# A fused attention and two-layer feed-forward kernel: GpSimd's subtractions and normalisations moved to VectorE in halves, another spacing of the y forms, and another order of the tail's joins

## The chip, the cores and the metric

The kernel runs on one core of a Trainium2 chip. A core has TensorE (PE in the profile: matmul; PEld: its weight load), VectorE (DVE), ScalarE (ACT), GpSimd (POOL) and SyncE (SP), which here issues the DMA transfers. Each engine works through its own queue in program order and waits on semaphores for the others. The metric is the device time of one execution in microseconds (us), as the median of several runs.

## What is computed

```python
# attention: q, k, v of shape (8 batches, 8 heads, 576 rows, 64)
q_s = softmax of q over the 64 columns of a row
k_s = exp(k - max over the 576 rows), divided by its sum over the rows
kv  = einsum('bhsd,bhse->bhde', k_s, v)
x   = einsum('bhsd,bhde->bhse', q_s, kv)      # -> 4608 tokens x 512
# first layer
g, val = x @ w_gate, x @ w_val                # 512 -> 1536
y = (g * sigmoid(g) * val) @ w_out            # 1536 -> 512
# second layer
h = y @ w_in                                  # 512 -> 1024
solu = h * softmax(h)
out = (layernorm(solu) * g_ln) @ w_out2       # 1024 -> 512
```

Each float32 product is made of three matmuls of a high and a low part (lines 938 to 940 of the kernel before).

## The kernel before

The work has three parts. A **prologue** does the attention of the first batch. Then nine **blocks** of 512 tokens run the first layer. Block 0 also converts the weights as they arrive. In blocks 1 to 7 the order of the work is written by hand: TensorE's products of a block are numbered in gaps, three for each n (12 matmuls each): gap 3n is the gate product of feature tile n (`wg`), gap 3n+1 the output product of tile n-2 (`y<-a,wo`), gap 3n+2 the value product of tile n (`wv`). `tasks_of(j)` says ahead of which gap every other task of the block is issued. Last come 18 **pairs** of the second layer, each with seven products of block matrices in the order 1, 6, 5, 2, 7, 3, 4 (`emit_pair`), whose sums are put together on VectorE.

Beside the products of tile n there are three steps: ScalarE's sigmoid form `st` from `wg` (L971), VectorE's product `st` with `wv` (L976), and the split into a high part on ScalarE (`a`, L980) and a low part on VectorE (`a`, L982). The text calls them st(n) and a(n). The product `y<-a,wo` of tile n needs a(n).

Beside them a block prepares the next batch and stores y:

- k, in two groups of four heads (`kv_max_rows` L511, `kv_max_all` L523 to L545, `kv_exp` L606, `kv_mm` L615). VectorE finds the column maxima and spreads them (`mt`, L539); the subtraction `kt - mt` (L545) is done by GpSimd in four pieces of 96x384; ScalarE's exp needs another function table than its sigmoid, so a table load stands ahead of it. The subtraction stands at gaps 5 and 20, the exp at 9 and 24, the matmuls `pk` at 11 and 26.
- q (`q_max` L685 and L688 at gap 8, `q_exp` L696 at 12, `q_norm` L702 to L708 at 14, `q_turn` at 18). Reductions are VectorE's, the subtraction (L688) and the normalisation (L708) GpSimd's, four pieces of 128x512 each. Later `q_split` (L761, L766) makes `qhl`, and `x_mm` (`px`, L786 to L788) the x of the next block.
- y in seven forms (`y_form`): some are sums of quarters of y (`yz`, L902, VectorE), each is split into a high part (ScalarE, L920) and a low part (VectorE, L922) in a tile `yf` with two buffers, and stored (L924). They start at gaps 5, 6, 12, 13, 14, 15, 16.
- one of the second layer's weights: `join_w2` (L320, L324) at gap 23.

In the tail, `h_first` copies product 1 from PSUM (`c`, L1343, ScalarE), `h_u` and `h_w` add products 6 and 5 to it (`uw`, L1347 and L1351), `h_other` makes `hh` (L1358). `emit_join_low` and `emit_join_high` put a transposed tile together again after its DMA (`zt<-wT`, L1430 on VectorE, L1433 on ScalarE), `emit_parts` splits it (L1441 ScalarE, L1444 VectorE), `emit_store` scales the output (L1481).

Of the kernel before, what the change touches and what calls it, by code (L numbers as in the profile page):

```python
# [19 lines left out]
P = 128  # L20
# [28 lines left out]
class Task:  # L49
# [7 lines left out]
    def step(self):  # L57
        before, Task.current = Task.current, self
        try:
            if self.g is None:  # L60
                self.g = self.f(*self.a)
                if self.g is None:
                    self.done = True
                    return None
            return next(self.g)
        except StopIteration:
            self.done = True
            return None
        finally:
            Task.current = before  # L70

    def finish(self):
        while not self.done:
# [132 lines left out]
def attention_glu_solu_kernel(  # L206
# [46 lines left out]
    def f32(ap):  # L253
        return ap.bitcast(F32)
# [18 lines left out]
            for t in kv_parts[b, p]:  # L273
                nc.gpsimd.memset(f32(t), 0.0)

    yf_dram = dram.tile([NT2 // 2, P, 2, 7, 2 * P], F32, name="yf_dram")
    NS = 8
    w1_dram = dram.tile([NS, P, 2, 2, DM], F32, name="w1_dram")
    x2_dram = dram.tile([KD, P, DF2], F32, name="x2_dram")
# [213 lines left out]
            )  # L493
        vt_t[b, h0] = vt

    def pieces(eng, start, stop):

        n = 1 if eng is nc.gpsimd else stop - start
        return [slice(x, x + n) for x in range(start, stop, n)] if n else []

    km_t, kt_exp, kt_sub = {}, set(), set()

    def kv_max(pool, b, h0, split=0):
        kv_max_rows(pool, b, h0)
        kv_max_all(pool, b, h0, split)

    def kv_max_rows(pool, b, h0):
        raw = kt_t[b, h0][0]
# [3 lines left out]
                out=m, in0=m if c > 1 else raw[:, 0], in1=raw[:, c], op=ALU.max  # L512
            )

    def kv_max_all(pool, b, h0, split=0):

        raw, kt = kt_t[b, h0]
        m = km_t.pop((b, h0))
        kt_sub.add((b, h0))
        N = HG * D  # L520
        NQ = SP // 32
        r = stat.tile([SP, N // 32], F32, tag="r", bufs=1, name="r")
        nc.vector.tensor_reduce(  # L523
            out=r, in_=m.rearrange("p h (e j) -> p (h e) j", j=32), axis=AX.X, op=ALU.max,
            apply_transpose=True,
        )
        r2 = stat.tile([32, N // 32, NQ], F32, tag="r2", bufs=1, name="r2")
        for a in range(NQ):
            nc.vector.tensor_copy(out=r2[:, :, a], in_=r[32 * a:32 * (a + 1), :])
        r3 = stat.tile([32, N // 32], F32, tag="r3", bufs=1, name="r3")  # L530
        nc.vector.tensor_reduce(out=r3, in_=r2, axis=AX.X, op=ALU.max)
        mb = tmp.tile([SP, N // 32, 32], F32, tag="st", bufs=3, name="mb")
        for a in range(NQ):
            nc.vector.tensor_copy(
                out=mb[32 * a:32 * (a + 1)],
                in_=r3.rearrange("p (n o) -> p n o", o=1).to_broadcast([32, N // 32, 32]),
            )
        mt = stat.tile([SP, 1, HG, D], F32, tag="m", bufs=1, name="mt")
        nc.vector.transpose(  # L539
            out=mt.rearrange("p o h d -> p (o h d)"), in_=mb.rearrange("p n j -> p (n j)")  # L540
        )
        yield
        for eng, s in ((nc.vector, slice(0, split)), (nc.gpsimd, slice(split, HG))):
            for s in pieces(eng, s.start, s.stop):
                eng.tensor_tensor(  # L545
                    out=kt[:, :, s, :], in0=raw[:, :, s, :],
                    in1=mt[:, :, s, :].to_broadcast([SP, KC, s.stop - s.start, D]),
                    op=ALU.subtract,
                )

    kT_t, kx_t = {}, {}

# [123 lines left out]
            need(q_at.get((j, h), 0) == n - 1)  # L676
            q_at[j, h] = n

    def q_max(pool, j, hs, eng=nc.gpsimd):
        q_step(j, hs, 1)  # L680
        placed(qt_t, j)
        raw, qt = (t[:, :, hs, :] for t in qt_t[j])
        n, nc_, nh = qt.shape[:3]
        qm = stat.tile([n, nc_, nh, 1], F32, tag="qm", bufs=2, name="qm")
        nc.vector.tensor_reduce(out=qm[:, :, :, 0], in_=raw, axis=AX.X, op=ALU.max)  # L685
        yield d["km"]
        for s in pieces(eng, 0, nc_):
            eng.tensor_tensor(  # L688
                out=qt[:, s], in0=raw[:, s],
                in1=qm[:, s].to_broadcast([n, s.stop - s.start, nh, D]), op=ALU.subtract,  # L690
            )

    def q_exp(j, hs):
# [1 line left out]
        qt = qt_t[j][1][:, :, hs, :]  # L695
        nc.scalar.activation(out=qt, in_=qt, func=AF.Exp)  # L696

    def q_norm(pool, j, hs, eng=nc.gpsimd):
        qt = qt_t[j][1][:, :, hs, :]
        n, nc_, nh = qt.shape[:3]  # L700
        qs = stat.tile([n, nc_, nh, 1], F32, tag="qs", bufs=2, name="qs")
        nc.vector.tensor_reduce(out=qs[:, :, :, 0], in_=qt, axis=AX.X, op=ALU.add)  # L702
        nc.vector.tensor_scalar_add(out=qs, in0=qs, scalar1=1e-9)
        nc.vector.reciprocal(out=qs, in_=qs)
        q_step(j, hs, 3)
        yield d["km"]
        for s in pieces(eng, 0, nc_):
            eng.tensor_tensor(  # L708
                out=qt[:, s], in0=qt[:, s],
                in1=qs[:, s].to_broadcast([n, s.stop - s.start, nh, D]), op=ALU.mult,  # L710
            )

    qT_t = {}
# [102 lines left out]
    def tasks_of(j):  # L816

        t = {}
        b = j + 1
        if b < B:
            for n, (load, rows, sub, exp, mm) in enumerate(((0, 2, 5, 9, 11), (12, 17, 20, 24, 26))):
                h0 = n * HG
                if n:
                    at(t, load, kv_load, att, b, h0)
                    at(t, load, v_load, att, b, h0)  # L830
                at(t, rows, kv_max_rows, att, b, h0)
                at(t, sub, kv_max_all, att, b, h0)
                at(t, exp, kv_exp, b, h0)
                for u in range(2):
                    at(t, mm, kv_mm, ps_at, att, b, h0, u)
        at(t, 15, lambda: w2_raw[j - 1].start())
        at(t, 23, join_w2, j - 1)
        at(t, 24, parts_of_w2, j - 1)
        if j + 1 < NB:
            at(t, 8, q_max, att, j + 1, ALLH)  # L840
            at(t, 12, q_exp, j + 1, ALLH)
            at(t, 14, q_norm, att, j + 1, ALLH)
            at(t, 18, q_turn, att, j + 1)
            at(t, 24, x_tiles, ph1x, j + 1)
            for p in range(NPAIR):
                at(t, 27 + p, q_split, att, j + 1, p)
                at(t, 29 + p, x_mm, ps_at, j + 1, p)
            at(t, 27, kv_next, j + 1)
            at(t, 33, q_next, j + 1)
        y_forms_at(t, j - 1)  # L850
        for e, f in enumerate(STREAM):
            if f is not None:
                at(t, 3 * f + 2, stream_next, j, e)
        at(t, 24, store_w2, j - 1)
        at(t, 25, stream_next, j, STREAM.index(None))
        return t
# [49 lines left out]
    def y_form(j, n):  # L906


        i, x, with_ = Y_FORMS[n]
        of = lambda n, r: y_quarter(j, n, r)  # L910
        if with_:
            if x and with_[0]:
                yz[j] = att.tile([P, 2, KH, P], F32, tag="z", bufs=1, name="yz")
            y_sum(yz[j], of, x, with_)
            s = yz[j]
        else:
            s = of(*x)
        f = att.tile([P, 2, 2, KH * P], F32R, tag="qhl", bufs=2, name="yf")
        h, l = (f[:, n].rearrange("p q (k t) -> p q k t", k=KH) for n in range(2))
        nc.scalar.copy(out=h, in_=s)  # L920
        yield
        nc.vector.tensor_tensor(out=l, in0=s, in1=f32(h), op=SUB)  # L922
        for q in range(2):
            nc.sync.dma_start(out=yf_dram[2 * j + q, :, :, i], in_=f32(f[:, :, q]))  # L924

    def y_forms_at(t, j):


        tasks = [Task(y_form, (j, n)) for n in range(7)]
        for n, g in enumerate((5, 6, 12, 13, 14, 15, 16)):  # L930
            at(t, g, tasks[n].step)
            at(t, g + 1, tasks[n].finish)

# [345 lines left out]
    def y_load(p):  # L1279
# [2 lines left out]

        for n in range(2):
            nc.sync.dma_start(
                out=f32(yq[p][n]).rearrange("p i k t -> p (i k t)"),
                in_=yf_dram[p, :, n].rearrange("p i w -> p (i w)"),
            )

    def y_make(p, n):
# [11 lines left out]
        f = tmp.tile([P, 2, KH, P], F32R, tag="st", bufs=3, name="yf")  # L1301
        nc.scalar.copy(out=f[:, 0], in_=s)
        nc.vector.tensor_tensor(out=f[:, 1], in0=s, in1=f32(f[:, 0]), op=SUB)
        nc.sync.dma_start(out=yf_dram[p, :, :, i], in_=f32(f).rearrange("p n k t -> p n (k t)"))

    t = tasks_of(NB - 1)
    at(t, 0, x_load)
# [190 lines left out]
    def emit_pair(p):  # L1498
# [6 lines left out]
        if p == 2:  # L1505
            h_first(p)
            emit_join_low(a)
            emit_join_high(a)
        if p > 1:
            emit_store(a - 1)  # L1510
            emit_parts(a, 0)
        if p == 0 or p > 2:
            h_first(p)
        product(p, 6)
        if p > 1:
            emit_join_low(b)
            emit_join_high(b)
        h_u(p)
        if p == 1:
            emit_join_low(a)  # L1520
            emit_join_high(a)
        product(p, 5)
        if p > 1:
            emit_parts(a, 1)
            emit_parts(b, 0)
        h_w(p)
        product(p, 2)
        h_11(p)
        product(p, 7)
# [109 lines left out]
```

## Time and profile before

| | |
|---|---|
| median of 3 runs | 1392.57 us (1392.31 to 1393.76) |
| the profiled execution | 1392.51 us, of which 1390.6 us from the first to the last instruction |
| TensorE busy | 1348.8 us (97%), weight loads 1110.7 us (80%) |
| VectorE busy | 835.2 us (60%) |
| ScalarE busy | 691.2 us (50%) |
| GpSimd busy | 164.6 us (12%) |
| mean granted TensorE clock | 0.988 of full speed |

A share is an average over the whole span. An engine with a small share can still be the one that another waits for at some place. TensorE's 97% leaves some 42 us in which it is idle, and the larger part of them lies in the prologue and in block 0: it is busy for 71.73 of the first 100 us.

### The profile page before, as it was taken

What the parts mean: (1) busy time and instruction counts of PE and PEld (TensorE: products, weight loads), DVE (VectorE), ACT (ScalarE), POOL (GpSimd) and SP (SyncE); (2) the same over time, 40 slices, a digit from 0 to 9 for tenths busy, and PEclk for the clock granted to TensorE, in tenths of its full rate; (3) what the DMA queues carried; (4) which work ended last, traced back from release to release, by engine and by line L of the source; (5) the groups of instructions that cost most, each with busy time, mean ns of one, the idle gap of its engine ahead of it and who ended that gap; (6) DMA issues with size and microseconds to landing.
All of it is one profiled execution on the core that took longest, in us unless ns stands there. A gap on an engine that the chain in (4) does not pass through costs nothing. (4 is left out here: it accounts for less than half of the span.)

```text
span 1390.6 us, 17771 instructions
## 1 busy us (share of the span) xinstructions
PE 1348.8 (97%) x6705; PEld 1110.7 (80%) x6705; DVE 835.2 (60%) x1407; ACT 691.2 (50%) x963; POOL 164.6 (12%) x196
## 2 busy tenths in 40 slices
PE   7769999999999999999999999999999999999998
PEld 6558888888888788888888788888887888888887
DVE  5868746446446545545645625445287787787774
ACT  5766434435434425425525524433157666667764
POOL 4000023022021121122112102000000000000000
PEclk8979999999999999999999999999999999999999
DMA  9983676756856656665666664656546766766651
GB/s 272 279 283 90 173 212 153 186 174 163 173 174 165 164 169 174 174 175 167 172 192 162 197 182 153 181 170 209 181 138 165 204 176 170 184 182 180 167 128 47
DMA packets 280741, 245.49 MB, mean 177 GB/s; under 512 B 210640, under 2 KB 257232, under 8 KB 269904
## 3 DMA queue, kind: packets, MB, share of 16 engines
q1 hardware_dynamic: 280656, 244.36, 62.6%
q8 instruction: 53, 0.87, 0.3%
q14 instruction: 32, 0.26, 0.1%
HBM read 162.01 MB, written 57.15 MB: 158 GB/s over the span
## 5 line engine op out<-in xcount | busy, mean ns | idle before, releaser
L980 ACT CAST a<-st 128x512 fp32r<-128x512 f32 x108 | 66.9, 620 | 274.6 <-DVE st L976 273.8
L976 DVE TENSOR_TENSOR st<-st,wv 128x512 f32<-128x512 f32 x108 | 73.8, 683 | 211.7 <-PE wv L940 208.5
L938 PE MATMUL wg<-xh,wgv 128*128 128x512 f32 x432 | 172.4, 399 | 12.1 <-ACT wgv L335 11.5
L939 PE MATMUL wg<-xl,wgv 128*128 128x512 f32 x432 | 170.3, 394 | 0.9 <-DVE xl L793 0.9
L939 PE MATMUL y<-a,wo 128*128 128x512 f32 x432 | 169.1, 391 | 2.1 <-DVE a L982 2.1
L938 PE MATMUL y<-a,wo 128*128 128x512 f32 x432 | 169.0, 391 | 1.9 <-ACT a L980 1.9
L940 PE MATMUL wg<-xh,wgv 128*128 128x512 f32 x432 | 170.0, 394 | 0.8 <-DVE wgv L345 0.7
L940 PE MATMUL y<-a,wo 128*128 128x512 f32 x432 | 168.7, 391 | 0.0
L938 PE MATMUL wv<-xh,wgv 128*128 128x512 f32 x432 | 168.5, 390 | 0.0
L940 PE MATMUL wv<-xh,wgv 128*128 128x512 f32 x432 | 168.1, 389 | 0.0
L939 PE MATMUL wv<-xl,wgv 128*128 128x512 f32 x432 | 168.1, 389 | 0.0
L982 DVE TENSOR_TENSOR a<-st,a 128x512 fp32r<-128x512 f32 x108 | 78.7, 728 | 71.9 <-ACT a L980 71.8
L1473 PE MATMUL y<-w,zhl 128*128 128x512 f32 (+1 forms) x296 | 113.6, 384 | 0.0
L1475 PE MATMUL y<-w,zhl 128*128 128x512 f32 (+1 forms) x296 | 113.5, 383 | 0.0
L1474 PE MATMUL y<-w,zhl 128*128 128x512 f32 (+1 forms) x296 | 113.5, 383 | 0.0
L938 PEld LDWEIGHTS wg<-xh,wgv 128*128 128x128 f32 x432 | 82.2, 190 | 30.2 <-ACT wgv L335 11.9
L545 POOL TENSOR_TENSOR kt<-kt,mt 96x384 f32<-96x384 f32 x48 | 61.2, 1302 | 358.8 <-DVE mt L539 358.8
L971 ACT ACTIVATE st<-wg 128x512 f32<-128x512 f32 x108 | 64.5, 597 | 72.8 <-PE wg L940 72.5
L940 PEld LDWEIGHTS wg<-xh,wgv 128*128 128x128 f32 x432 | 82.1, 190 | 19.2 <-DVE wgv L345 1.9
L938 PEld LDWEIGHTS y<-a,wo 128*128 128x128 f32 x432 | 81.5, 189 | 19.4 <-ACT a L980 2.7
L939 PEld LDWEIGHTS y<-a,wo 128*128 128x128 f32 x432 | 81.5, 189 | 19.3 <-DVE a L982 2.7
L939 PEld LDWEIGHTS wg<-xl,wgv 128*128 128x128 f32 x432 | 82.4, 191 | 17.9 <-DVE xl L793 1.7
(264 smaller groups left out, 2557.7 us busy)
## 6 DMA issues: line engine op xcount, KB each, us to landing
wgv<-w_dram SPq DMA_DIRECT2D x64, 1024.0 KB, 5.3
yf_dram<-yf SPq DMA_DIRECT2D x126, 256.0 KB, 2.8
yh<-yf_dram SPq DMA_DIRECT2D x18, 896.0 KB, 4.8
yl<-yf_dram SPq DMA_DIRECT2D x18, 896.0 KB, 6.8
vt<-in_v_dram SPq DMA_DIRECT2D x64, 144.0 KB, 4.5
out_dram<-ot SPq DMA_DIRECT2D x35, 256.0 KB, 2.9
w_dram<-wgv SPq DMA_DIRECT2D x8, 1024.0 KB, 8.3
kt<-in_k_dram SPq DMA_DIRECT2D x56, 144.0 KB, 5.6
```

Of the source, the lines that this page charges most:

```text
L545: eng.tensor_tensor(out=kt[:, :, s, :], in0=raw[:, :, s, :], in1=mt[:, :, s, :].to_broadcast([SP, KC, s.stop - s.start, D]), op=ALU.subtract,)
L938: nc.tensor.matmul(out=po, lhsT=wh, rhs=rh, start=start, stop=False, **k)
L939: nc.tensor.matmul(out=po, lhsT=wh, rhs=rl, start=False, stop=False, **k)
L940: nc.tensor.matmul(out=po, lhsT=wl, rhs=rh, start=False, stop=stop, **k)
L971: nc.scalar.activation(out=st, in_=pg, func=AF.Silu)
L976: nc.vector.tensor_tensor(out=st, in0=st, in1=pv, op=ALU.mult)
L980: nc.scalar.copy(out=ah, in_=st)
L982: nc.vector.tensor_tensor(out=al, in0=st, in1=f32(ah), op=ALU.subtract)
L1473: nc.tensor.matmul(out=po[:, s], lhsT=zh[:, c, :], rhs=wh[:, s], start=first, stop=False)
L1474: nc.tensor.matmul(out=po[:, s], lhsT=zh[:, c, :], rhs=wl[:, s], start=False, stop=False)
L1475: nc.tensor.matmul(out=po[:, s], lhsT=zl[:, c, :], rhs=wh[:, s], start=False, stop=last)
```

## The change

Five parts:

- **k.** The subtraction of a group is done by VectorE in two halves (96 partitions x 768 elements each), both one gap after the maxima, gaps 6 and 21.
- **q.** In blocks the subtraction and the normalisation are VectorE's too, each in two halves of 128x1024: the subtraction at gaps 9 and 10, the sums at 13, the normalisation at 14 and 15.
- **The prologue's q** stays on GpSimd, with one instruction of 128x4x256 where there were four of 128x256.
- **y forms** start at gaps 4, 6, 8, 11, 12, 14, 16. A form is stored by one transfer of 512 KB where there were two of 256 KB; `yf_dram` is laid out anew, and `y_load` of the tail reads seven runs of 1 KB for each partition where it read one of 7 KB.
- **Tail.** `h_first` stands ahead of `emit_parts` and `emit_store`, `emit_store` behind `emit_parts`; the join of b stands behind `h_u` and product 5 (for pair 2 behind `h_w` too).

```diff
-    yf_dram = dram.tile([NT2 // 2, P, 2, 7, 2 * P], F32, name="yf_dram")
+    yf_dram = dram.tile([NB, 7, P, 2, 2, 2 * P], F32, name="yf_dram")
...
-        for eng, s in ((nc.vector, slice(0, split)), (nc.gpsimd, slice(split, HG))):
-            for s in pieces(eng, s.start, s.stop):
-                eng.tensor_tensor(
-                    out=kt[:, :, s, :], in0=raw[:, :, s, :],
-                    in1=mt[:, :, s, :].to_broadcast([SP, KC, s.stop - s.start, D]),
-                    op=ALU.subtract,
-                )
+        for s in range(0, HG, step):
+            s = slice(s, s + step)
+            nc.vector.tensor_tensor(
+                out=kt[:, :, s, :], in0=raw[:, :, s, :],
+                in1=mt[:, :, s, :].to_broadcast([SP, KC, step, D]), op=ALU.subtract,
+            )
...
-                at(t, sub, kv_max_all, att, b, h0)
+                a = Task(kv_max_all, (att, b, h0))
+                at(t, sub, a.next)
+                at(t, sub + 1, a.finish)
...
-            at(t, 8, q_max, att, j + 1, ALLH)
+            m = Task(q_max, (att, j + 1, ALLH, nc.vector, 2))
+            n = Task(q_norm, (att, j + 1, ALLH, nc.vector, 2))
+            at(t, 8, m.next)
+            at(t, 9, m.next)
+            at(t, 10, m.finish)
             at(t, 12, q_exp, j + 1, ALLH)
-            at(t, 14, q_norm, att, j + 1, ALLH)
+            at(t, 13, n.next)
+            at(t, 14, n.next)
+            at(t, 15, n.finish)
...
-        for q in range(2):
-            nc.sync.dma_start(out=yf_dram[2 * j + q, :, :, i], in_=f32(f[:, :, q]))
+        nc.sync.dma_start(out=yf_dram[j, i], in_=f32(f))
...
-        for n, g in enumerate((5, 6, 12, 13, 14, 15, 16)):
+        for n, g in enumerate((4, 6, 8, 11, 12, 14, 16)):
...
-                out=f32(yq[p][n]).rearrange("p i k t -> p (i k t)"),
-                in_=yf_dram[p, :, n].rearrange("p i w -> p (i w)"),
+                out=f32(yq[p][n]).rearrange("p i k t -> p i (k t)"),
+                in_=yf_dram[p // 2, :, :, n, p % 2].rearrange("i p w -> p i w"),
...
             emit_join_high(a)
+            emit_parts(a, 0)
+        elif p > 2:
+            h_first(p)
+            emit_parts(a, 0)
+        elif p == 0:
+            h_first(p)
         if p > 1:
             emit_store(a - 1)
-            emit_parts(a, 0)
-        if p == 0 or p > 2:
-            h_first(p)
         product(p, 6)
-        if p > 1:
-            emit_join_low(b)
-            emit_join_high(b)
         h_u(p)
...
         product(p, 5)
+        if p == 2:
+            h_w(p)
         if p > 1:
+            emit_join_low(b)
+            emit_join_high(b)
             emit_parts(a, 1)
             emit_parts(b, 0)
-        h_w(p)
+        if p != 2:
+            h_w(p)
```

TensorE's order is the same in both kernels. What moves stands in the queues of VectorE, ScalarE, GpSimd and SyncE. Three places follow; a line number is that of the kernel the row is from.

VectorE in block 3, from the low part of the third y form to the second normalisation half, before (L976 and L982 are st(4) and a(4), then L702 to L704 the sums of q):

```order
L922 TENSOR_TENSOR yf<-yt,yf 128x512
L902 TENSOR_TENSOR yz<-yt 128x512
L976 TENSOR_TENSOR st<-st,wv 128x512
L982 TENSOR_TENSOR a<-st,a 128x512
L702 TENSOR_REDUCE qs<-qt 128x32
L703 TENSOR_SCALAR qs<-qs 128x32
L704 RECIPROCAL qs<-qs 128x32
L922 TENSOR_TENSOR yf<-yz,yf 128x512
L902 TENSOR_TENSOR yz<-yz,yt 128x512
```

The same place in the change (L980 and L986 are st(4) and a(4), L699 to L701 the sums of q, L706 the normalisation halves, L907 `yz`, L927 `yf`):

```order
L907 TENSOR_TENSOR yz<-yt 128x512
L927 TENSOR_TENSOR yf<-yz,yf 128x512
L907 TENSOR_TENSOR yz<-yz,yt 128x512
L699 TENSOR_REDUCE qs<-qt 128x32
L700 TENSOR_SCALAR qs<-qs 128x32
L701 RECIPROCAL qs<-qs 128x32
L927 TENSOR_TENSOR yf<-yz,yf 128x512
L980 TENSOR_TENSOR st<-st,wv 128x512
L986 TENSOR_TENSOR a<-st,a 128x512
L706 TENSOR_TENSOR qt<-qt,qs 128x1024
L907 TENSOR_TENSOR yz<-yt,yz 128x512
L706 TENSOR_TENSOR qt<-qt,qs 128x1024
```

The sums of q and one form now stand ahead of st(4) and a(4), and the normalisation halves stand behind a(4), between forms. Between these and a(5) there follow one `yf`, one `yz` and st(5).

VectorE in block 3 at the second k group, before (L539 makes `mt`; L976 and L982 are st(7) and a(7)):

```order
L534 COPY mb<-r_3626 32x256 x3
L539 STREAM_TRANSPOSE mt<-mb 96x256
L976 TENSOR_TENSOR st<-st,wv 128x512
L982 TENSOR_TENSOR a<-st,a 128x512
L320 SCALAR_TENSOR_TENSOR w2r2r<-w2r2r 128x1024
```

and in the change (L543 is the subtraction):

```order
L532 COPY mb<-r_3571 32x256 x3
L537 STREAM_TRANSPOSE mt<-mb 96x256
L543 TENSOR_TENSOR kt<-kt,mt 96x6x128 x2
L980 TENSOR_TENSOR st<-st,wv 128x512
L986 TENSOR_TENSOR a<-st,a 128x512
L323 SCALAR_TENSOR_TENSOR w2r2r<-w2r2r 128x1024
```

The two halves stand between `mt` and st(7). Ahead of this place, from a(5) to `mt`, VectorE's rows are the same in both: the row maxima of k, a `yf`, a copy `qw`, st(6), a(6), and the steps from the maxima to `mt`.

VectorE in pair 2 of the tail, before (L1430 are the joins of a and b, L1347 is `h_u`, L1351 `h_w`, L1358 `hh`):

```order
L1430 COPY zt<-wT 128x1024 x2
L1347 TENSOR_TENSOR uw<-c_8164,h 128x512
L1444 TENSOR_TENSOR zhl<-zt,zhl 128x1024
L1351 TENSOR_TENSOR uw<-uw,h 128x512
L1358 TENSOR_TENSOR hh<-uw,h 128x512
```

and in the change (L1434 joins, L1351 `h_u`, L1355 `h_w`, L1362 `hh`):

```order
L1434 COPY zt<-wT 128x1024
L1351 TENSOR_TENSOR uw<-c_8044,h 128x512
L1355 TENSOR_TENSOR uw<-uw,h 128x512
L1434 COPY zt<-wT 128x1024
L1448 TENSOR_TENSOR zhl<-zt,zhl 128x1024
L1362 TENSOR_TENSOR hh<-uw,h 128x512
```

Both sums stand ahead of the second join now, which waits for a DMA; the first `hh` still stands behind a split of the joined tile.

## Rows read from the trace of the kernel before

**Rows 1.** Busy time of each engine in a stretch, granted clock, DMA share, GB/s.
```profile
100.00:1034.00 934.00, 927.07 (x4705) 767.80 (x4704) 496.86 (x835) 396.39 (x565) 130.94 (x117) 1.00 0.61 171
```

**Rows 2.** TensorE's waits: engine line <- releaser, us in total, times, longest.
```profile
PE wg L938 <- ACT wgv L335: 11.5, 1, 11.5
PE pk L615 <- ACT kt L606: 6.1, 6, 1.6
...
PE y L724 <- POOL qt L708: 2.5, 1, 2.5
...
PE h L938 <- DVE hh L1358: 1.3, 3, 0.9
...
PE h L938 <- DVE uw L1347: 0.9, 1, 0.9
...
PE h L938 <- ACT c L1343: 0.7, 2, 0.5
...
PE px L787 <- DVE qhl L766: 0.5, 2, 0.3
```

**Rows 3.** Timeline around block 3's second k group: start, duration, [idle before <- releaser].
```profile
450.84 0.44 DVE L539 STREAM_TRANSPOSE mt<-mb 96x256 f32<-96x256 f32 x1
451.21 0.65 DVE L976 TENSOR_TENSOR st<-st,wv 128x512 f32<-128x512 f32 x1
...
451.36 5.37 POOL L545 TENSOR_TENSOR kt<-kt,mt 96x384 f32<-96x384 f32 x4 [15.41 <-DVE mt L539]
...
452.42 0.59 ACT L971 ACTIVATE st<-wg 128x512 f32<-128x512 f32 x1
453.03 1.28 ACT L606 ACT_TABLE_LOAD   x1
456.76 1.48 ACT L606 ACTIVATE kt<-kt 96x1536 f32<-96x1536 f32 x1 [2.45 <-POOL kt L545]
...
456.28 0.39 PE L940 MATMUL wv<-xh,wgv 128*128 128x512 f32 x1
458.30 1.74 PE L615 MATMUL pk<-vt,kt 96*64 96x65 f32 x48 [1.63 <-ACT kt L606]
```

**Rows 4.** TensorE's timeline behind that wait.
```profile
459.97 0.80 PE L938 MATMUL wg<-xh,wgv 128*128 128x512 f32 x1
...
463.40 0.39 PE L940 MATMUL wg<-xh,wgv 128*128 128x512 f32 x1
```

**Rows 5.** Timeline of block 3 between the y forms and a(5).
```profile
424.53 0.68 DVE L902 TENSOR_TENSOR yz<-yt 128x512 f32<-128x512 f32 x1
...
426.67 0.69 DVE L982 TENSOR_TENSOR a<-st,a 128x512 fp32r<-128x512 f32 x1 [0.74 <-ACT a L980]
427.28 2.28 DVE L702 TENSOR_REDUCE qs<-qt 128x32 f32<-128x2048 f32 x1
...
430.74 1.41 DVE L902 TENSOR_TENSOR yz<-yz,yt 128x512 f32<-128x512 f32 x1
...
441.07 0.62 ACT L920 CAST yf<-yz 128x512 fp32r<-128x512 f32 x1 [3.68 <-DMA yf_dram<-yf]
...
442.24 0.69 DVE L982 TENSOR_TENSOR a<-st,a 128x512 fp32r<-128x512 f32 x1 [2.80 <-ACT a L980]
...
442.99 0.51 PE L939 MATMUL y<-a,wo 128*128 128x512 f32 x1 [0.22 <-DVE a L982]
```

**Rows 6.** VectorE's subtraction of a whole k group in the first blocks, grouped by shape.
```profile
L545 DVE TENSOR_TENSOR kt<-kt,mt 96x1536 f32<-96x1536 f32 x2 | 3.5, 1754 | 0.1
```

**Rows 7.** TensorE around the first `px` of block 5.
```profile
680.29 0.39 PE L940 MATMUL wv<-xh,wgv 128*128 128x512 f32 x1
...
682.18 0.45 PE L938 MATMUL wg<-xh,wgv 128*128 128x512 f32 x1
```

**Rows 8.** Pair 2 of the tail around VectorE's second join.
```profile
1049.07 0.75 DVE L1430 COPY zt<-wT 128x1024 uint16<-128x1024 uint16 x1 [2.63 <-DMA wT<-w]
...
1050.44 0.50 PE L938 MATMUL h<-f,yh 128*128 128x512 f32 x1 [0.88 <-DVE uw L1347]
```

More of the change, by code (lines that the diff above doesn't have):

```diff
@@ L70, in step, with next @@
             Task.current = before
+    def next(self):
+        self.step()
     def finish(self):
@@ L494, in v_load, with kv_max @@
         vt_t[b, h0] = vt
-    def pieces(eng, start, stop):
-        n = 1 if eng is nc.gpsimd else stop - start
-        return [slice(x, x + n) for x in range(start, stop, n)] if n else []
     km_t, kt_exp, kt_sub = {}, set(), set()
-    def kv_max(pool, b, h0, split=0):
+    def kv_max(pool, b, h0, step=2):
         kv_max_rows(pool, b, h0)
-        kv_max_all(pool, b, h0, split)
+        kv_max_all(pool, b, h0, step)
     def kv_max_rows(pool, b, h0):
@@ L513, in kv_max_rows, with kv_max_all @@
             )
-    def kv_max_all(pool, b, h0, split=0):
+    def kv_max_all(pool, b, h0, step=2):
         raw, kt = kt_t[b, h0]
@@ L677, in q_step, with q_max @@
             q_at[j, h] = n
-    def q_max(pool, j, hs, eng=nc.gpsimd):
+    def q_max(pool, j, hs, eng=nc.gpsimd, step=4):
         q_step(j, hs, 1)
@@ L685, in q_max @@
         nc.vector.tensor_reduce(out=qm[:, :, :, 0], in_=raw, axis=AX.X, op=ALU.max)
-        yield d["km"]
-        for s in pieces(eng, 0, nc_):
+        for c in range(0, nc_, step):
+            yield d["km"]
+            c = slice(c, c + step)
             eng.tensor_tensor(
-                out=qt[:, s], in0=raw[:, s],
-                in1=qm[:, s].to_broadcast([n, s.stop - s.start, nh, D]), op=ALU.subtract,
+                out=qt[:, c], in0=raw[:, c], in1=qm[:, c].to_broadcast([n, step, nh, D]), op=ALU.subtract
             )
@@ L696, in q_exp, with q_norm @@
         nc.scalar.activation(out=qt, in_=qt, func=AF.Exp)
-    def q_norm(pool, j, hs, eng=nc.gpsimd):
+    def q_norm(pool, j, hs, eng=nc.gpsimd, step=4):
         qt = qt_t[j][1][:, :, hs, :]
@@ L705, in q_norm @@
         q_step(j, hs, 3)
-        yield d["km"]
-        for s in pieces(eng, 0, nc_):
+        for c in range(0, nc_, step):
+            yield d["km"]
+            c = slice(c, c + step)
             eng.tensor_tensor(
-                out=qt[:, s], in0=qt[:, s],
-                in1=qs[:, s].to_broadcast([n, s.stop - s.start, nh, D]), op=ALU.mult,
+                out=qt[:, c], in0=qt[:, c], in1=qs[:, c].to_broadcast([n, step, nh, D]), op=ALU.mult
             )
@@ L1303, in y_make @@
         nc.vector.tensor_tensor(out=f[:, 1], in0=s, in1=f32(f[:, 0]), op=SUB)
-        nc.sync.dma_start(out=yf_dram[p, :, :, i], in_=f32(f).rearrange("p n k t -> p n (k t)"))
+        nc.sync.dma_start(out=yf_dram[j, i, :, :, q], in_=f32(f).rearrange("p n k t -> p n (k t)"))
     t = tasks_of(NB - 1)
```

## The prediction

> **What bounds the kernel now.** I read the busy times first, then TensorE's waits, then the timeline at each of them. From 100 us to the end of the blocks TensorE is busy for 927.07 of 934 us at full clock while VectorE is busy for 53% of it [rows 1]. So TensorE bounds the kernel, and a change that leaves TensorE's order alone can only give back its waits or add new ones. The list of waits names them [rows 2]: the largest, 11.5 us for block 0's weights, is not touched. Then come six waits of `pk` for the exp of k, 6.1 us together, and six in the tail (for `hh` 1.3, `uw` 0.9, `c` 0.7). Everything else behind the prologue is under 1 us.
>
> A wait costs more than its idle time. Matmuls of 512 columns start 0.227 us apart (2.72 us for the 12 of a gap), but their rows last 0.39. In [rows 3] the last `wv` starts at 456.28 and `pk` at 458.30, 2.02 apart: 1.79 lost for an idle time of 1.63, so idle plus 0.16. In the tail the first matmul after a wait also holds up the next by 0.1: I count 0.28 there.
>
> Why is the exp late? [Rows 3] from the top: `mt` is ready at 451.28, GpSimd takes 5.37 us for four pieces (1.34 each), the exp starts the moment they end and lasts 1.48. ScalarE's table load is over at 454.31, ScalarE then idles 2.45 us. The last link ahead of `pk` is GpSimd's subtraction.
>
> **k's halves.** VectorE did the same subtraction whole in 1.754 us for 1536 elements [rows 6]; a tensor-tensor of 512 elements takes 0.68 [rows 5]. That is 1.05 ns an element and about 0.15 us an instruction, so two halves of 768 cost 1.9 us against GpSimd's 5.37. But they go into another queue: st(7) stood right behind `mt` (451.21) and now stands behind the halves. ScalarE's a(7), its st(8) (L971), the table load and then the exp follow st(7) in order. So I count back from when `pk` may start, 456.5: exp 1.48, table load 1.28, L971 0.59, the cast of a(7) 0.62, st(7) 0.65, halves 1.9 give 6.5 with nothing idle between. `mt` must be ready by about 449.9, against 451.28 now. Faster subtraction alone isn't enough; `mt` has to come 1.4 us sooner.
>
> It does, if a(5) does. In [rows 5] ScalarE's cast of a y form waited 3.68 us until 441.07 for the stores of an earlier form; a(5)'s cast was queued behind it, and VectorE had idled 2.80 us before a(5) at 442.24. From a(5)'s end (442.93) to `mt`'s (451.28) are 8.35 us of the same instructions before and after. The new spacing gives each of the two `yf` buffers over two gaps, 5.4 us, before it is needed again, where before forms came every 2.72; so that wait goes. What comes in its place is VectorE's own work. st(4) and a(4), which ended at 427.4 (426.67 + 0.69), now stand behind the sums of q (2.28, and some 0.5 for two small steps) and a 0.7 `yz`, 3.5 us more: a(4) ends at 430.9. Its product is gap 19. Gap 26 ended at 456.5, so gap 19 began at 456.5 less eight gaps of 2.72, 434.7, less the 0.7 lost between: 434.0. Margin 3.1. Behind a(4): normalisation halves 2 x 1.22, `yz` twice 0.69, `yf` 0.68, to 435.4; st(5), its cast and a(5) 2.0 more: 437.4, and 439.5 if ScalarE's queue (a function table, the joins' casts) costs 2. Needed at 442.2. Then `mt` is ready at 447.9 at the latest: 2 us of margin against 449.9, and the exp is over before `wv` ends. The six blocks look alike (waits 0.68 to 1.63), so the six waits go: 6.1 + 6 x 0.16 = **7.1**.
>
> In block 3 the granted clock dropped after the longest wait: TensorE was let down to the half level right behind it, and eight steps from 459.97 to 463.40 took 3.43 where 1.81 is usual [rows 4]. With the wait gone this goes: **1.6**.
>
> a(5)'s own wait in block 3, 0.22 idle on the low part and as much again around it [rows 5]: **0.5** (0.22 to 0.7).
>
> **q on VectorE.** GpSimd spent its time on it off the path; VectorE now takes four instructions of 1.22, 4.9 us a block, besides 3.8 for k: 8.7 of a block's 107 us, on an engine idle for 47%. So it costs nothing where it is in time; its cover is a(4)'s 3.1 us, the tightest. If that is gone, TensorE waits at gap 19 for each us beyond it. Both subtraction halves are done before st(2) and the exp at gap 12. Beyond that, `yz` beside GpSimd took 1.41 against 0.68 alone [rows 5], which falls away twice a block, 1.4 us.
>
> The Trainium skill, "SBUF — State Buffer", section "Who interferes with whom", says that a VectorE instruction with two SBUF inputs contends with a GpSimd instruction that reads SBUF, through an exclusive lock under which the loser blocks fully. The 1.41 agrees in kind; a full block by one piece of GpSimd's 1.34 would have made it up to 2.0 and the relief up to 2.7 a block. By either, only the margin moves, not the sum. [...]
>
> **px.** The first `px` of block 5: from 680.29 to 682.18 is 1.89 [rows 7] for 2048 columns' worth of matmuls (one of 512, three of 384, three of 128), 0.91 at 0.227 for 512. It waits for `qhl`, behind a(8), `pk`'s sums and the split in VectorE's and ScalarE's queues, which the weight joins, slowed by GpSimd, had pushed back. Without that they are about 2 us sooner against `wv`. Some of the 0.98 is usual at such a change of shape: 0.85 each, two blocks [rows 2]: **1.7** (0.5 to 2.0).
>
> **Tail.** Six waits, 1.3 + 0.9 + 0.7 = 2.9 idle, with 6 x 0.28 some 4.6. In pair 2 [rows 8] `uw` stood behind a join that waited for a DMA until 1049.07, and TensorE lost 0.88 idle until 1050.44; ahead of the join it needs only product 6, so this goes, as do the two for `c` and two of the three for `hh`. The wait for pair 2's first `hh` stays: it still stands behind the join's split, which the DMA sets, 0.9 + 0.28. So 4.6 - 1.2 = **3.4** (2.5 to 4.6). Later joins of b stay covered by the products that follow.
>
> **Transfers.** Seven fewer issues a block; 1 KB runs on reading. A pair's yh and yl are loaded while the pair before it is computed, and no wait for them stands among TensorE's, so I take nothing. If that cover goes, a pair waits for its first product by what the reading takes longer.
>
> **Prologue.** Coarser pieces on GpSimd: the wait of 2.5 for `qt` [rows 2] may grow by nothing or by as much again; block 0 then waits 11.5 us for weights whose arrival does not depend on it, so I take 0 (bound +2.5 if it moved the loads).
>
> **Sum.** 7.1 + 1.6 + 0.5 + 1.7 + 3.4 = 14.3 off the profiled 1392.51 (span 1390.6 and 1.9 around it; the median is 1392.57): **1378.2 us**.
>
> **The rivals.**
> *All waits go* (A), 1378.2, own range 1376 to 1381: chance 0.60. For it: margins of 2 to 3 us at each step.
> *VectorE's queue takes GpSimd's place* (B): a(5) isn't sooner, since the halves of q eat what the forms' spacing gives. Then `mt` is at 451.28, halves to 453.2, st(7), a(7)'s cast, L971 and table load to 456.4, exp to 457.9: 0.35 sooner than 458.24. So 6 x 0.35 = 2.1 of the 7.1, half of the clock's and `px`'s: 2.1 + 0.5 + 1.6 + 3.4 = 7.6, 1384.9. It decides from `mt` later than 449.9. Chance 0.20.
> *The tail's order does nothing* (C), as the transposing DMA ends last whatever stands ahead of it: 1378.2 + 3.4 = 1381.6. Against it, `uw` needs no DMA. Chance 0.10.
> *a(4) late, slower* (D): each us by which a(4) ends past 434.0 is one for TensorE at gap 19 in seven blocks; 2.5 us past it outweighs all 14.3 and gives 3.2 more (7 x 2.5 = 17.5), 1395.7, and a clock drop of 1.6 behind each such wait would make it 1407. It needs my walk to be off by 5.6 us. Chance 0.06.
> The rest, 0.04: gains met by a new loss of like size (prologue, loads), about 1392.
>
> **Numbers.** The time is A's, 1378.2. The range 1376 to 1386 takes in B and C, the bounds of `px` and of the tail; D and the rest, 0.10, lie outside. A measurement tells 0.2%, 2.8 us, from no change: faster is A, B and C, 0.90; the rest 0.04; slower 0.06.
>
> **What would show it.** In the trace after: no `pk` waiting for an exp from block 1 on, the exp beginning where its table load ends, and granted clock 1.00 at 460 us. `mt` of block 3 ready by 448, a(4) by 431. GpSimd without work in the blocks save for clearing. No wait for `c` or `uw` in the tail, and one for `hh`, in pair 2. I am wrong if TensorE waits at gap 19 for a(4) (D), if `pk` waits while ScalarE runs back to back from st(7) (B), or if a load of yh or yl is late.

## The result and the profile after

The changed kernel takes 1377.18 us (median of 4 runs, 1376.49 to 1378.42) against 1392.44 for the kernel before: a ratio of 0.9894, 95% interval 0.9877 to 0.9912, 15.3 us less. Its profiled execution took 1376.76 us with a span of 1374.9.

The page's busy times, and the stretch of [rows 1], after:

```profile
PE 1340.4 (97%) x6705; PEld 1107.4 (81%) x6705; DVE 869.1 (63%) x1459; ACT 692.2 (50%) x963; POOL 32.9 (2%) x80
```
```profile
100.00:1034.00 934.00, 934.00 (x4752) 775.55 (x4751) 538.45 (x908) 403.17 (x577) 2.93 (x15) 1.00 0.59 173
```

GpSimd's work in the blocks has gone to VectorE (GpSimd from 130.94 us to 2.93, VectorE from 496.86 to 538.45), and the profile shows no idle time of TensorE from 100 us to the blocks' end (934.00 of 934.00). The waits that answer to [rows 2], after:

```profile
PE wg L942 <- ACT wgv L338: 11.9, 1, 11.9
...
PE y L721 <- POOL qt L706: 2.5, 1, 2.5
...
PE h L942 <- DVE hh L1362: 0.7, 1, 0.7
```

`pk`, `px`, `uw` and `c` are not in TensorE's list any more; of the three waits for `hh` one is left, in pair 2. The timeline of block 3 that answers to [rows 3] and [rows 5], after (L986 low part of a, L925 and L984 ScalarE's casts of a form and of a, L537 `mt`, L543 the halves, L603 table load and exp):

```profile
427.06 0.69 DVE L986 TENSOR_TENSOR a<-st,a 128x512 fp32r<-128x512 f32 x1 [0.69 <-ACT a L984]
428.81 0.69 DVE L907 TENSOR_TENSOR yz<-yt,yz 128x512 f32<-128x512 f32 x1
...
430.78 0.39 PE L942 MATMUL y<-a,wo 128*128 128x512 f32 x1
...
434.10 0.63 ACT L925 CAST yf<-yz 128x512 fp32r<-128x512 f32 x1
434.61 0.64 ACT L984 CAST a<-st 128x512 fp32r<-128x512 f32 x1
...
435.28 0.69 DVE L986 TENSOR_TENSOR a<-st,a 128x512 fp32r<-128x512 f32 x1 [2.45 <-ACT a L984]
...
443.88 0.44 DVE L537 STREAM_TRANSPOSE mt<-mb 96x256 f32<-96x256 f32 x1
444.35 1.82 DVE L543 TENSOR_TENSOR kt<-kt,mt 96x768 f32<-96x768 f32 x2
446.10 0.68 DVE L980 TENSOR_TENSOR st<-st,wv 128x512 f32<-128x512 f32 x1
...
447.98 1.28 ACT L603 ACT_TABLE_LOAD   x1
449.27 1.49 ACT L603 ACTIVATE kt<-kt 96x1536 f32<-96x1536 f32 x1
...
452.31 0.39 PE L944 MATMUL wv<-xh,wgv 128*128 128x512 f32 x1
452.63 0.57 PE L612 MATMUL pk<-vt,kt 96*64 96x65 f32 x12
```

The reader is to see the distance of each step from the last `wv`, which starts at 452.31 here and at 456.28 in [rows 3]. `mt` is ready 8.0 us ahead of it (444.32), against 5.0 before (451.28): 3.0 sooner. The cast at 434.10 doesn't wait for a store. The exp ends at 450.76 and `pk` starts at 452.63, right behind `wv`: 1.87 us of margin where there was a wait. a(4) ends at 427.75, 3.03 us ahead of its product at 430.78.

**Where the time came from.** All kernels here have the same 6705 matmuls in the same order, so the start of the same matmul in two traces can be compared. I take three places: the 401st matmul (91.74 us before, behind block 0's wait for weights), one in the tail ahead of pair 2's waits (1047.81 before), and the last. What a kernel gains on the kernel before, in us of its profiled execution:

| kernel | to 91.74 | blocks | tail | at the last matmul |
|---|---|---|---|---|
| the change | 0.9 | 10.9 | 3.9 | 15.6 |
| k_only | -0.9 | 4.2 | 0.0 | 3.3 |
| q_only | -0.1 | -7.1 | 0.1 | -7.2 |
| forms_gaps | -1.8 | 10.9 | 0.3 | 9.5 |
| forms_odd | -0.6 | 10.9 | 0.4 | 10.7 |
| tail_only | 0.9 | 0.4 | 3.8 | 5.1 |
| forms_tail | 2.1 | 10.9 | 3.9 | 16.9 |
| forms_tail_pair2 | 1.1 | 10.9 | 3.0 | 15.0 |
| kq_old_forms | -0.1 | 3.1 | 3.0 | 6.0 |
| after_two_stores | 1.0 | 10.9 | 3.8 | 15.7 |
| sums_x2 | -1.4 | 4.2 | 3.9 | 6.7 |
| sums_x3 | -0.9 | -11.8 | 3.9 | -8.8 |

The first column differs by 3.8 us between executions, even among kernels whose start is the same (forms_gaps -1.8, forms_tail 2.1): it is noise of the start, and the change's 0.9 in it is not shown to be the change's. The blocks of the six kernels that have spaced forms and no wait left in them repeat to 0.1, those of the two with the old blocks (before and tail_only) to 0.4. The tail repeats to 0.4 within the old order and within the new one, with two exceptions in the new: forms_tail_pair2, which has another order again, and kq_old_forms. There VectorE's second join in pair 2 waited longer for its DMA than in the change, so the first `hh` was late by 1.5 us where it is late by 0.7. The join in the change and in kq_old_forms:

```profile
1037.35 0.77 DVE L1434 COPY zt<-wT 128x1024 uint16<-128x1024 uint16 x1 [1.27 <-DMA wT<-w]
```
```profile
1046.94 0.77 DVE L1434 COPY zt<-wT 128x1024 uint16<-128x1024 uint16 x1 [2.15 <-DMA wT<-w]
```

What made that DMA later is not shown; nor is how often it happens, with one trace of each kernel.

### The profile page after: what moved, and what is told of

It reads as the page before. It is cut to its first block, busy times and chain, and to the rows that moved or that the text cites. A ratio compares the mean times of both kernels' runs of the same rounds, so it can differ in the third digit from the quotient of the medians.

```text
span 1374.9 us, 17556 instructions
## 1 busy us (share of the span) xinstructions
PE 1340.4 (97%) x6705; PEld 1107.4 (81%) x6705; DVE 869.1 (63%) x1459; ACT 692.2 (50%) x963; POOL 32.9 (2%) x80
## 4 chain that ended last, share of the span: by engine, by line
PE 92%; DMA 3%; DVE 2%; SPq 1%; ACT 1%; issue 0%; ACTq 0%
PE wg L942 7%; PE y L942 7%; PE y L943 7%; PE y L944 7%; PE wg L944 7%; PE wg L943 7%; PE wv L942 7%; PE wv L943 7%; PE wv L944 7%; PE y L1478 4%; PE y L1479 4%; PE y L1477 4%; PE h L942 4%; PE h L943 4%; PE h L944 4%; PE pk L612 2%
## 5 line engine op out<-in xcount | busy, mean ns | idle before, releaser
L984 ACT CAST a<-st 128x512 fp32r<-128x512 f32 x108 | 67.0, 620 | 323.0 <-DVE st L980 322.9
L980 DVE TENSOR_TENSOR st<-st,wv 128x512 f32<-128x512 f32 x108 | 74.1, 686 | 200.4 <-PE wv L944 195.6
L986 DVE TENSOR_TENSOR a<-st,a 128x512 fp32r<-128x512 f32 x108 | 74.7, 692 | 76.8 <-ACT a L984 76.7
L943 PEld LDWEIGHTS y<-a,wo 128*128 128x128 f32 x432 | 81.4, 188 | 18.7 <-DVE a L986 2.2
L942 PEld LDWEIGHTS y<-a,wo 128*128 128x128 f32 x432 | 81.4, 188 | 18.6 <-ACT a L984 2.0
L944 PEld LDWEIGHTS y<-a,wo 128*128 128x128 f32 x432 | 81.4, 188 | 17.0
```

The source lines that it names most:

```text
L942: nc.tensor.matmul(out=po, lhsT=wh, rhs=rh, start=start, stop=False, **k)
L943: nc.tensor.matmul(out=po, lhsT=wh, rhs=rl, start=False, stop=False, **k)
L944: nc.tensor.matmul(out=po, lhsT=wl, rhs=rh, start=False, stop=stop, **k)
L980: nc.vector.tensor_tensor(out=st, in0=st, in1=pv, op=ALU.mult)
L984: nc.scalar.copy(out=ah, in_=st)
L986: nc.vector.tensor_tensor(out=al, in0=st, in1=f32(ah), op=ALU.subtract)
```

## The experiments

**One part at a time.** Each of these four is the kernel before with one part of the change. My theory was that the y forms' spacing makes `mt` early, and that this is what frees `pk`; the rival was that the subtraction itself, on GpSimd, is the cause.

*k_only*: k's halves on VectorE.

```diff
-        for eng, s in ((nc.vector, slice(0, split)), (nc.gpsimd, slice(split, HG))):
-            for s in pieces(eng, s.start, s.stop):
+        for s in (slice(0, split),) if split else (slice(0, 2), slice(2, HG)):
+            if True:
+                eng = nc.vector
...
-                at(t, sub, kv_max_all, att, b, h0)
+                a = Task(kv_max_all, (att, b, h0))
+                at(t, sub, a.next)
+                at(t, sub + 1, a.finish)
```

> The kernel before with k's subtraction alone moved to VectorE in halves. Theory (the path to the exp is set by when mt is ready, and the y forms' spacing is what makes it early): mt of block 3 stays at about 451, the halves push st(7), the cast of a(7) and the table load back, the exp starts 0.3 to 0.4 us sooner than before, so pk still waits about 1 us in each of six blocks; 2 to 4 us faster than before, about 1389.5. Rival (the time of the subtraction itself is the cause): all six waits go, 7 to 9 us faster, about 1384.

Measured: 1387.20 us against 1391.43 on the same chip, ratio 0.9970 (0.9958 to 0.9982), between the two theories. TensorE's wait, the timeline of block 3, and the stretch behind the wait (the last three figures are granted clock, DMA share and GB/s), here and in the kernel before:

```profile
PE pk L619 <- issue: 3.5, 6, 1.1
```
```profile
451.23 1.82 DVE L549 TENSOR_TENSOR kt<-kt,mt 96x768 f32<-96x768 f32 x2
452.97 0.68 DVE L982 TENSOR_TENSOR st<-st,wv 128x512 f32<-128x512 f32 x1
...
454.82 1.28 ACT L610 ACT_TABLE_LOAD   x1
456.11 1.49 ACT L610 ACTIVATE kt<-kt 96x1536 f32<-96x1536 f32 x1
...
457.70 1.51 PE L619 MATMUL pk<-vt,kt 96*64 96x65 f32 x42 [1.13 <-issue]
```
```profile
460.00:464.00 4.00, 4.00 (x19) 3.29 (x18) 1.92 (x7) 2.85 (x6) 0.00 (x0) 1.00 0.99 307
```
```profile
460.00:464.00 4.00, 4.00 (x12) 3.20 (x12) 1.99 (x8) 2.52 (x5) 0.14 (x1) 0.60 0.98 319
```

The queue is as the prediction's rival B had it: halves, st(7), a(7)'s cast, L977, table load, exp, with nothing idle between. The subtraction ends at 453.05, sooner than GpSimd's, yet the exp waits for the table load behind st(7). Six waits remain, 3.5 us where 6.1 were. The list names no releaser for them ("issue"), but the exp ends at 457.60 and `pk` starts at 457.70. What the theory left out is the clock: here it stayed at the full level behind block 3's wait (1.00, against 0.60 before), and with it some 1.6 us of the blocks' 4.2 came back. That the shorter wait (1.13 us for 1.63) is the reason is not shown, and q_only speaks against length alone.

*q_only*: q's subtraction and normalisation on VectorE (the change's lines of `q_max`, `q_norm` and `tasks_of`; the prologue keeps its pieces).

```diff
-            at(t, 8, q_max, att, j + 1, ALLH)
+            m = Task(q_max, (att, j + 1, ALLH, nc.vector, 2))
+            n = Task(q_norm, (att, j + 1, ALLH, nc.vector, 2))
+            at(t, 8, m.next)
+            at(t, 9, m.next)
+            at(t, 10, m.finish)
...
-            at(t, 14, q_norm, att, j + 1, ALLH)
+            at(t, 13, n.next)
+            at(t, 14, n.next)
+            at(t, 15, n.finish)
```

> The kernel before with q's subtraction and normalisation alone moved to VectorE in halves. Theory: the two halves of the normalisation (2.4 us) stand ahead of a(5) and mt while two yz beside GpSimd win back 1.4; mt is about 1 us later, pk waits about 1 us longer in six blocks; 3 to 8 us slower, about 1397. Rival (VectorE is idle for 47% of a block, so the work is absorbed): within 1 us of before.

Measured: 1398.38 against 1391.43, ratio 1.0048 (1.0029 to 1.0067): slower, as the theory had it. TensorE's wait for the exp:

```profile
PE pk L618 <- ACT kt L609: 10.1, 6, 1.7
```

10.1 us where 6.1 were, and a second half-level stretch, behind the wait of block 2, besides that of block 3. Most of the rest of the 7.1 us, some 1.4, is small waits for a(5) in five blocks. The stretches behind the waits of blocks 1, 2 and 4:

```profile
247.00:251.00 4.00, 4.00 (x44) 3.37 (x40) 2.35 (x9) 1.82 (x5) 0.14 (x1) 1.00 0.99 341
354.00:358.00 4.00, 4.00 (x36) 3.25 (x32) 2.32 (x10) 1.87 (x5) 0.14 (x1) 0.59 1.00 330
571.00:575.00 4.00, 4.00 (x48) 3.41 (x43) 2.23 (x9) 1.78 (x6) 0.14 (x1) 1.00 0.97 323
```

The six waits here are all of one length, 1.64 to 1.71 us, yet the clock fell behind two of them (blocks 2 and 3) and not behind the other four. The length of the wait does not decide it by itself.

An engine idle for 47% of the blocks did not absorb 2.4 us, because they came ahead of `mt`.

*forms_gaps*: the spacing of the y forms.

```diff
-        for n, g in enumerate((5, 6, 12, 13, 14, 15, 16)):
+        for n, g in enumerate((4, 6, 8, 11, 12, 14, 16)):
```

> The kernel before with the y forms alone moved to gaps 4, 6, 8, 11, 12, 14, 16 (two transfers each as before, GpSimd keeps its work). Theory: ScalarE's cast of a form no longer waits for a store, a(5) and mt come 2 to 3 us sooner, GpSimd's 5.4 us then end before the last wv does: the six waits of pk, the half-level stretch and a(5)'s wait go, 8 to 11 us faster, about 1383. Rival (GpSimd's subtraction is the cause): only a(5)'s wait in block 3 goes, under 1 us, about 1392.

Measured: 1382.10 against 1391.43, ratio 0.9932 (0.9916 to 0.9949): the theory's value. The timeline of block 3, GpSimd still at work, then ScalarE's waits for the stores in the kernel before, and last the same here:

```profile
432.96 1.42 DVE L902 TENSOR_TENSOR yz<-yt 128x512 f32<-128x512 f32 x1
...
445.90 0.44 DVE L539 STREAM_TRANSPOSE mt<-mb 96x256 f32<-96x256 f32 x1
...
446.42 4.38 POOL L545 TENSOR_TENSOR kt<-kt,mt 96x384 f32<-96x384 f32 x4 [10.13 <-DVE mt L539]
...
451.89 1.49 ACT L606 ACTIVATE kt<-kt 96x1536 f32<-96x1536 f32 x1
...
455.25 0.92 PE L615 MATMUL pk<-vt,kt 96*64 96x65 f32 x24
```
```profile
ACT yf L920 <- DMA yf_dram<-yf: 21.2, 8, 3.7
```
```profile
ACT yf L920 <- DMA yf_dram<-yf: 4.5, 2, 3.5
```

With `mt` at 446.34, GpSimd is done at 450.80, before the table is loaded, and the exp ends 1.87 us ahead of `pk`. This one line gives the whole of the blocks' 10.9, and place by place the same gains as the change (to 0.1 us). The two `px` lose nothing here either, with GpSimd at work.

*tail_only*: the change's `emit_pair`.

```diff
+        elif p > 2:
+            h_first(p)
+            emit_parts(a, 0)
...
-        if p > 1:
-            emit_join_low(b)
-            emit_join_high(b)
         h_u(p)
...
         if p > 1:
+            emit_join_low(b)
+            emit_join_high(b)
```

> The kernel before with the tail's new order alone. Theory: the waits for c and uw and two of the three for hh go, 2.5 to 4 us faster, about 1389. Rival (the transposing DMA ends last whatever stands ahead of it): no change, 1392.4.

Measured: 1387.01 against 1391.43, ratio 0.9971 (0.9960 to 0.9982). The trace gives 3.8 us in the tail and one wait for `hh` (0.6 us), with the blocks as they were.

**Is the work on VectorE needed?** *forms_tail* is the kernel before with the last two of these edits and no other.

> The kernel before with the y forms' gaps and the tail's order alone; GpSimd keeps all of k's and q's work, two transfers for each form. Theory (the spacing of the forms is what frees pk, GpSimd's work then ends in time): all of the change's gain without moving any work to VectorE, 1377.5 to 1379. Rival (VectorE's halves add something of their own): 2 us or more above the changed kernel's 1377.2.

Measured: 1378.03 (1375.52 to 1378.50), ratio 0.9905 (0.9889 to 0.9922), the change's 0.9894 within the interval; blocks 10.9 and tail 3.9, as the change. So the moves to VectorE, the one transfer and the new layout add nothing that can be measured. (The blocks agree to 0.01 us in these traces since TensorE has no wait left in them; that says nothing of the margins.) *after_two_stores* is the change with the old layout:

```diff
-        nc.sync.dma_start(out=yf_dram[j, i], in_=f32(f))
+        for q in range(2):
+            nc.sync.dma_start(out=yf_dram[2 * j + q, :, :, i], in_=f32(f[:, :, q]))
```

> The changed kernel with a form stored by two transfers of 256 KB into the old layout, read in one run of 7 KB for each partition. Theory (the transfers are hidden either way): within 1 us of the changed kernel, 1377. Rival (two issues and two landings hold a buffer longer, so a cast waits for a store again): 2 us slower or more, with ScalarE waits for the stores in the trace.

Measured: 1376.61 (1376.52 to 1379.10), ratio 0.9898 (0.9883 to 0.9913). The transfers are hidden either way.

**Is the spacing needed?** *kq_old_forms* is the change with the forms at their old gaps.

```diff
-        for n, g in enumerate((4, 6, 8, 11, 12, 14, 16)):
+        for n, g in enumerate((5, 6, 12, 13, 14, 15, 16)):
```

> The changed kernel with the y forms back at gaps 5, 6, 12, 13, 14, 15, 16. Theory: ScalarE's cast of a form waits for a store again and the halves of q stand ahead of a(5), so mt of block 3 is at 451 to 452 and pk waits 1 to 1.5 us in each of six blocks; with the tail's gain kept about 1390, 10 to 14 us slower than the changed kernel. Rival (the work on VectorE is what removed the waits): within 2 us of the changed kernel.

Measured: 1385.83, ratio 0.9959 (0.9944 to 0.9974), 8.6 us above the change and less than I expected. TensorE's waits, and ScalarE's cast of the last form in block 3:

```profile
PE pk L612 <- issue: 4.4, 6, 1.1
...
PE px L784 <- DVE qhl L763: 0.5, 2, 0.3
```
```profile
441.00 0.62 ACT L925 CAST yf<-yz 128x512 fp32r<-128x512 f32 x1 [3.95 <-DMA yf_dram<-yf]
```

The wait for the store is back, and with it `mt` at 451.22, as in [rows 3]. I had put the halves of q on top; they hide under the 3.95 us for which ScalarE waits anyway, so the waits are near those of k_only, 0.7 each and not 1 to 1.5. The two `px` wait as before, though GpSimd has no work in the blocks. In its trace, 0.9 us of the loss are the tail's late DMA named above.

**Distance or position?** In *forms_odd* the forms are two gaps apart, and the last is a gap later than before.

```diff
-        for n, g in enumerate((5, 6, 12, 13, 14, 15, 16)):
+        for n, g in enumerate((5, 7, 9, 11, 13, 15, 17)):
```

> The kernel before with the y forms two gaps apart but none ended sooner: gaps 5, 7, 9, 11, 13, 15, 17. Theory (it is the distance between forms that share two buffers, not how early they are): no cast waits for a store, mt of block 3 is some 3 us sooner, no pk waits; 8 to 11 us faster than before, about 1383. Rival (it is that the last forms are done by gap 16): pk waits as before, 1391.

Measured: 1381.64, ratio 0.9929 (0.9914 to 0.9943); blocks 10.9 again, and one cast that waits 3.4 us for a store. So it is the distance between the forms and not how early the last one is. A third buffer, which would take the wait away by itself, was not tried.

**How near was VectorE to being the bound?** *sums_x2* and *sums_x3* are the change with q's sums taken two and three times, 2.28 and 4.56 us more ahead of a(4).

```diff
         nc.vector.tensor_reduce(out=qs[:, :, :, 0], in_=qt, axis=AX.X, op=ALU.add)
+        for _ in range(1 if eng is nc.vector else 0):
+            nc.vector.tensor_reduce(out=qs[:, :, :, 0], in_=qt, axis=AX.X, op=ALU.add)
```

> The changed kernel with q's sums in a block taken twice, 2.28 us more of VectorE's time ahead of st(4) and a(4) in seven blocks, 16 us in all. Theory (a(4) has 3 us of margin, and a(5) waits for ScalarE behind it): a(4) of block 3 ends some 0.8 us ahead of its product, TensorE waits nowhere new, 1377 to 1378. Rival (the margin is nearly used up): a wait at gap 19 in each block, 1385 or more.

> The changed kernel with q's sums taken three times, 4.56 us more ahead of a(4) in seven blocks. Theory: a(4) ends 1.5 us after its product could start; 7 x 1.8 is some 12 us, and a half-level stretch of about 1.6 us behind some of these waits may come on top: 1389 to 1400. Rival (an engine idle for 37% of its time takes it): 1377 to 1379.

Measured: 1384.71 (ratio to before 0.9946, 0.9931 to 0.9961) and 1400.57 (1.0059, 1.0042 to 1.0076), 7.5 and 23.4 us above the change. The first was misjudged, and the second lies just above its range. TensorE's wait and the timeline of block 3 in sums_x2:

```profile
PE pk L612 <- issue: 2.7, 6, 0.5
```
```profile
434.37 0.69 DVE L988 TENSOR_TENSOR a<-st,a 128x512 fp32r<-128x512 f32 x1 [0.69 <-ACT a L986]
...
435.77 0.39 PE L944 MATMUL y<-a,wo 128*128 128x512 f32 x1
...
456.56 1.49 ACT L603 ACTIVATE kt<-kt 96x1536 f32<-96x1536 f32 x1
...
458.15 1.24 PE L612 MATMUL pk<-vt,kt 96*64 96x65 f32 x33 [0.46 <-issue]
```

a(4) is in time, by 0.71 us (435.06 to 435.77), as the theory had it. But the exp is late, by 0.46. I had thought that the delay would end at a(5), for which VectorE waits 2.45 us on ScalarE in the change. It doesn't: ScalarE's casts there follow VectorE's `yz`, so ScalarE is late by the same 2.28 us. And 1.4 us are lost once near 133 us, at the end of block 0, where the extra sum delays `kvl`; the two `px` wait again and cost 0.75 each. In sums_x3 the waits for a(4) come too, and those for the exp grow:

```profile
PE y L944 <- ACT a L986: 7.2, 7, 2.6
PE pk L612 <- issue: 6.8, 6, 1.2
...
PE y L945 <- DVE a L988: 2.9, 7, 1.6
```

Its loss lies on both: about 1.6 us at gap 19 and 1.3 at `pk` in each of six blocks, 3.7 at the end of block 0, and 0.8 for each `px`.

**The last wait of the tail.** *forms_tail_pair2* puts the join and the split of b behind the first `hh` in pair 2.

```diff
         h_other(p, 3, 1, 3)
+        if p == 2:
+            emit_join_low(b)
+            emit_join_high(b)
+            emit_parts(b, 0)
```

> The kernel before with the forms' gaps and the tail's order, and in pair 2 the join and split of b behind the first hh. Theory: the last wait for hh in the tail, 0.8 us, goes and nothing else moves: 1377.2, no more than the noise below the version without it. Rival (b's split is then late for the products that read it): TensorE waits for zhl instead, no gain or a loss of 1 us.

Measured: 1377.52 (1376.89 to 1381.99), ratio 0.9904 (0.9885 to 0.9923). The wait goes, and a pair later there is a new one, which costs 1.8 us where 0.9 were won (tail 3.0 and not 3.9):

```profile
1060.78 0.50 PE L938 MATMUL h<-ft,yh 128*128 128x512 f32 x1 [1.44 <-DVE hh L1358]
```

There VectorE's second join waited 1.90 us for its DMA, against 0.31 in forms_tail, and the second sum and `hh` stand behind it. Whether the edit made that DMA late or chance did is not shown. The times don't tell the two kernels apart.

No version beat the change by anything measurable; forms_tail equals it with a fraction of its edits.

## Why the prediction was right, point by point

- **The sum**: 14.3 us off, 15.3 measured, 15.6 in the traces, of which 0.9 lie in the noisy start. Blocks 10.9 by the terms (7.1, 1.6, 0.5, 1.7), 10.9 measured (6.8, 1.6, 0.7, 1.7), the small misses against each other. The six waits cost some 0.12 each above their idle time, not 0.16; in part since `pk` without a wait starts 0.32 behind `wv` (452.31 to 452.63), where the count took 0.227. None of the 14.3 needed the work moved to VectorE (forms_tail), and the prediction didn't see that.
- **k**: shown. The path named (store, cast, a(5), `mt`, halves, st(7), table load, exp) is the one that k_only and kq_old_forms are held up on, and forms_gaps and forms_odd free it alone. The prediction's walk along the queues said 2 us of margin at `pk`, and 1.87 is in the trace; 3.1 at a(4), and 3.03. `mt` came 3.0 us sooner against `wv`, where the walk had 3.4: it held `pk`'s start at 456.5, though `wv` itself comes 0.7 sooner when a(5) holds nothing up. The two halves took 1.82 for 1.9, little more than the whole at 1.754, so the 0.15 for each instruction was too much.
- **Clock**: the half-level stretch of [rows 4] is gone, 1.6 us in the traces for 1.6. The prediction tied it to the wait ahead of it; that it goes with the wait is what was seen, but not every wait of that length has one behind it (q_only). The granted clock behind `pk` in block 3 of the change:

```profile
453.00:457.00 4.00, 4.00 (x56) 3.47 (x52) 2.31 (x8) 1.27 (x4) 0.14 (x1) 1.00 0.94 307
```

- **a(5)**: 0.7 between the same matmuls, for 0.5.
- **px**: the size was right, 1.7 for 1.7, and the reason was not. [Rows 7] took 1.89, and the same place takes 1.04 after (671.37 for the last `wv`, 672.41 for `wg`); block 6 gains 0.83 likewise. The prediction blamed weight joins that GpSimd slowed. But in forms_gaps and forms_odd GpSimd keeps its work and `px` doesn't wait, and in kq_old_forms GpSimd has none and it does. In the traces of all thirteen kernels `px` waits in just those in which `pk` waits for the exp; how the one leads to the other was not followed. That the size came out is luck.
- **q**: costs nothing in the change, but the step "its cover is a(4)'s 3.1 us, the tightest" failed. sums_x2 shows that in blocks 1 to 6 `mt`'s is tighter, 1.9 us, a number that stood in the same text, and that the end of block 0 has less still: of a delay of 2.28 us it passed on 1.4, so by estimate it covers 0.8. q_only shows what q costs with that cover gone: 7.1 us.
- **Contention**: `yz` takes 0.69 in the change, where GpSimd is idle, and 1.42 in forms_gaps, where it works; both gain 10.9 in the blocks, so it moves only margins, as said. The Trainium skill, "SBUF — State Buffer", section "Who interferes with whom", has an exclusive lock, under which the loser blocks fully. The trace agrees that both are held up: GpSimd's four pieces took 5.37 in [rows 3] beside two-input work of VectorE, 4.38 in forms_gaps with less of it, and in the kernel before all 14 `yz` beside GpSimd took 1.41 us, the other 18 took 0.69. Whether one waits for the whole instruction of the other these rows don't tell.
- **Tail**: 3.9 against 3.4, in six traces of this order 3.8 to 3.9 and in a seventh 3.0; the five waits that went cost some 0.3 above their idle time each, priced at 0.28, and the one that stayed was priced at 0.9 idle instead of 0.7. **Transfers and prologue**: nothing that stands out of the noise, as said.
- **A reading that was wrong**: "everything else behind the prologue is under 1 us" left out two waits for the split of `st` in block 0, 1.9 and 1.8 us. They stay in the change (1.5 and 1.8), so the sum doesn't feel it.
- **The rivals**: B was real, only not here. k_only and kq_old_forms are it, with 3.5 and 4.4 us of waits left. B's sum counted a(5)'s 0.5 as gained, though in it a(5) isn't sooner; in kq_old_forms that wait stayed (0.23 idle). D is sums_x3: its 4.56 us are 1.5 more than a(4)'s margin, and 1.6 were lost at gap 19 in each of six blocks; no half-level stretch stood behind any of these waits.

## What to carry to other kernels

A stall that shows at one engine (GpSimd, the releaser of the last wait) can be set by a wait three steps upstream on others: count back from the time at which the result is needed and ask which earlier step could start sooner. Work moved onto an engine with idle time is free only as far as the shortest margin of anything queued behind it, which its share of busy time doesn't tell. Where one of two engines waits for the other, ask what the other had waited for, before the wait is counted as slack.

## What the runs showed of the hardware

- Behind some of the longest waits of TensorE in the blocks the granted clock was at its half level (1.2 GHz): after 1.63 us of idle time in the kernel before, 1.60 in tail_only, 1.70 and 1.64 in q_only. It stayed at the full level behind four other waits of 1.64 to 1.71 in q_only, behind 2.71 at the end of block 0 in sums_x3, and behind the 1.13 of k_only. What decides it was not tried.
- The start of the kernel, up to its 401st matmul, varied by 3.8 us between executions, the blocks by 0.1 where no wait was left in them and by 0.4 in two traces of the old blocks; a gain of 1 us in the blocks can be read from one trace, but not from the times.
- A transposing DMA of the tail kept VectorE waiting 1.27 us in one execution and 2.15 at the same place in another with the same order of the tail; TensorE lost 0.9 us by it.
